# The first DMA requests of a fused attention and GLU kernel: wq in two contraction halves, in turn with x tiles 2 and 3

## The chip, the cores and the metric

The kernel runs on one core of a Trainium2 chip. The metric is the device time of one execution in microseconds. Six runs of the kernel before gave a median of 232.52 us, from 232.12 to 233.14.

A core has engines that run side by side and wait for each other through semaphores: PE (matrix products, with PEld for its weight loads), DVE (vector), ACT (scalar functions), POOL, and SP, which in this kernel only issues DMA requests.

## The reference, cut to what matters

The input x has 2048 rows of 512. It is normalized, and the result goes into two branches whose outputs are multiplied and added to x:

```python
xn = _layernorm(x, axis=-1)
s = _A_ref(xn, A_wqkv, A_wo)                  # qkv = xn @ wqkv, local attention
g = _silu(_B_ref(xn, B_w_gate, B_w_up, B_w_down))   # gelu(xn @ w_gate) * (xn @ w_up) @ w_down
return x + s * g
```

The attention has 32 heads of 16; each row attends to 8 rows, at distances 0, 2, ..., 14 behind it. wqkv is 512 x 1536: 512 columns each for q, k and v. The GLU is 1792 wide. All inputs are bf16.

## The kernel before, in words

The sequence is cut into 4 blocks of 512 rows (index j), and each block into 4 tiles of 128 rows. For a block the kernel makes, in this order on PE: q, k and v; the gate and up products of the GLU, 14 chunks (`glu`); then the down projection and the output, tile by tile (`down`). Attention's elementwise products run on DVE beside these. The program order on each engine is written out by hand (line 51), so an instruction that waits holds everything behind it on its engine.

The loads are all issued by SP, at the head of the program (lines 93 to 101): x tiles 0 to 3, one request of 128 KB each (`load_x`, line 82); then wqkv in three requests of 512 KB, q's 512 columns, k's, v's (`load_w`, line 88); then x tiles 4 to 7 in one request, halves of w_gate and w_up, and the rest of x. A request for wq, wk or wv brings for each of the 128 partitions four pieces of 512 columns, one for each contraction block of 128 rows (index k in `load_w`, dk in `project`).

The start is lines 472 to 496. PE runs 17 matmuls on zeros. For each of the first four tiles DVE computes mean and variance (`first_moments`, lines 176 and 177), ACT takes a square root (line 178), DVE the reciprocal (line 183) and the normalized tile xn (line 198). PE transposes xn in four pieces into PSUM (line 207), and the result is copied to xnT, by ACT for tiles 0 and 1 (line 216) and by DVE for tiles 2 and 3 (line 218). Tile 1's copy has two parts: contraction blocks 0 and 1, then 2 and 3.

DVE's order at the start is: moments of tiles 0 and 1, normalization of 0 and 1 (PE's transposes go beside it), then moments of tiles 2 and 3, then normalization of 2 and 3.

The first QKV matmuls (lines 486 to 489, through `project`, line 241) make q for tiles 0 and 1, 256 columns of rows at once, in four PSUM buffers: first contraction blocks 0 and 1 for all four outputs, eight matmuls, then blocks 2 and 3 for all four, eight more:

```python
    for dks in ((0, 1), (2, 3)):
        for fo in range(NC):
            project(qs[fo], wqkv_sb, fo * P, 0, 0, HQ, dks)
```

Then come the transposes of tile 2, the first k output, the transposes of tile 3, the other k outputs for tiles 0 and 1 (lines 492 to 496), q and k for tiles 2 and 3, and v for all four tiles (lines 500 to 505). The q and k results are copied to SBUF by ACT (lines 259 and 262). v goes through memory (lines 265, 267) and comes back in another layout (`load_v`, line 275).

Of the kernel before, what the change touches and what calls it, by code (L numbers as in the profile page):

```python
# [13 lines left out]
P = 128  # L14
# [14 lines left out]
def kernel(  # L29
# [14 lines left out]
    B, S, D = A_x.shape  # L44
    DF = B_w_gate.shape[1]
    NT, NC, NF, NJ = S // P, D // P, DF // P, S // TQ
    TPQ = TQ // P
# [27 lines left out]
    wqkv_sb = wts.tile([P, NC, 3 * D], BF16, name="wqkv_sb")  # L75
# [6 lines left out]
    def load_x(t, n=1):  # L82
        nc.sync.dma_start(  # L83
            out=x_sb[:, t : t + n, :],
            in_=x2d[t * P : (t + n) * P, :].rearrange("(t p) d -> p t d", p=P),
        )

    def load_w(dst, src, lo, hi):
        nc.sync.dma_start(
            out=dst[:, :, lo:hi], in_=src.rearrange("(k p) n -> p k n", p=P)[:, :, lo:hi]  # L90
        )

    for t in range(TPQ):
        load_x(t)
    for i in range(3):
        load_w(wqkv_sb, A_wqkv, i * D, (i + 1) * D)
    load_x(TPQ, TPQ)
    for i, (lo, hi) in enumerate(((0, DF // 2), (DF // 2, DF))):
        load_w(wg_sb, B_w_gate, lo, hi)
        load_w(wu_sb, B_w_up, lo, hi)  # L100
        load_x((2 + i) * TPQ, TPQ)

    def load_late_weights():
# [15 lines left out]
        out=vT.rearrange("(k p) n -> p k n", p=P)[:, :, 0:PAD],  # L119
        in_=warm[:, 0 : NC * PAD].rearrange("p (k n) -> p k n", k=NC),  # L120
# [426 lines left out]
```

The softmax here doesn't subtract the row's maximum and nothing guards it: scores larger than these inputs give would overflow.

## Time and profile before

| | |
|---|---|
| median of six runs | 232.52 us (232.12 to 233.14) |
| profiled execution: its time | 232.24 us |
| its span, first to last instruction | 230.5 us |
| PE busy | 225.0 us (98%) |
| DVE busy | 146.9 us (64%) |
| ACT busy | 132.2 us (57%) |
| granted PE clock | 0.999 |

Times inside the span count from its start. A line of a timeline gives start, duration, engine, line of the kernel, operation, what is written from what, the number of instructions merged into the line, and in square brackets how long the engine was idle before it and what ended that. The chain of waits is followed back from the last instruction: at each step to what released it. Durations of consecutive instructions on one engine overlap a little, since an engine starts one before the last is out of it.

SP's requests at the start, from the timeline: the four x tiles go out from 0.80 to 2.62 us, the three parts of wqkv from 2.66 to 4.19, x tiles 4 to 7 at 4.23, the first half of w_gate at 4.78, the first half of w_up at 5.44.

### The profile page before, as it was taken

The numbers are of one execution on the slowest core, as the hardware profiler recorded it, in microseconds if no ns is written. First come the engines' busy times: TensorE is split into PE (matmuls) and PEld (weight loads), VectorE is DVE, ScalarE is ACT, GpSimd is POOL, SyncE is SP. The second block draws the span as 40 slices with busy tenths as digits, with TensorE's granted clock in tenths as the row PEclk, the third lists the DMA queues.
The fourth block names the chain that finished last, engine by engine and source line by source line (L and its number), as shares of the span: only waits on it lengthen the run. The fifth ranks groups of instructions, "written<-read, shape, count | busy, mean of one in ns | idle before, by whom it ended". The sixth has DMA issues, their size and how long they took to land.

```text
span 230.5 us, 3545 instructions
## 1 busy us (share of the span) xinstructions
PE 225.0 (98%) x1339; PEld 106.3 (46%) x1339; DVE 146.9 (64%) x234; ACT 132.2 (57%) x219; POOL 22.1 (10%) x61
## 2 busy tenths in 40 slices
PE   7999999999999999999999999999999999999993
PEld 5865444444444444444444444444444444444453
DVE  5693996897795198981677149951449429864132
ACT  3779869755413865756621595656741386576211
POOL 1058933000000000130000000000000000000000
PEclk9999999999999999999999999999999999999999
DMA  5999499821378211100277611000046810000001
GB/s 167 362 375 367 108 214 216 278 69 48 103 173 200 50 29 23 26 0 0 92 173 163 140 24 31 18 11 0 28 136 160 203 30 0 0 0 4 23 23 46
DMA packets 27057, 23.71 MB, mean 103 GB/s; under 512 B 6688, under 2 KB 27040, under 8 KB 27040
## 3 DMA queue, kind: packets, MB, share of 16 engines
q1 hardware_dynamic: 27040, 23.49, 38.7%
q8 instruction: 10, 0.16, 0.3%
q14 instruction: 7, 0.06, 0.1%
HBM read 18.22 MB, written 4.21 MB: 97 GB/s over the span
## 4 chain that ended last, share of the span: by engine, by line
PE 93%; DVE 3%; DMA 2%; SPq 1%; ACT 0%; issue 0%; DVEq 0%
PE g_ps L241 21%; PE y_ps L398 21%; PE u_ps L241 20%; PE qkv_ps L241 17%; PE s_ps L408 6%; PE L_ps L297 3%; PE o_ps L357 3%; DVE pv L343 2%; DMA wqkv_sb<-in_A_wqkv_dram 2%; SPq L83 1%; PE tr L207 1%; DVE h L386 0%; PE sp_ps L332 0%; PE den_ps L317 0%; ACT ge L382 0%
## 5 line engine op out<-in xcount | busy, mean ns | idle before, releaser
L241 PE MATMUL g_ps<-xnT,wg_sb 128*128 128x512 bf16 x224 | 57.6, 379 | 0.0
L241 PE MATMUL u_ps<-xnT,wu_sb 128*128 128x512 bf16 x224 | 57.5, 379 | 0.0
L398 PE MATMUL y_ps<-wd_sb,h 128*128 128x512 bf16 (+1 forms) x238 | 51.2, 366 | 0.0
L386 DVE TENSOR_TENSOR h<-ge,u 128x512 bf16<-128x512 bf16 x56 | 23.7, 424 | 34.1 <-ACT u L384 33.9
L287 DVE TENSOR_TENSOR pk<-q_sb,k_sb 128x2048 bf16<-128x2048 bf16 x32 | 37.8, 1220 | 11.5 <-ACT k_sb L262 11.5
L241 PE MATMUL qkv_ps<-xnT,wqkv_sb 128*128 128x512 bf16 (+1 forms) x224 | 43.0, 349 | 0.4 <-DMA wqkv_sb<-in_A_wqkv_dram 0.4
L382 ACT ACTIVATE ge<-g_ps 128x512 bf16<-128x512 f32 x56 | 33.6, 601 | 14.4 <-PE g_ps L241 12.9
L384 ACT ACTIVATE u<-u_ps 128x512 bf16<-128x512 f32 x56 | 33.6, 600 | 13.9 <-PE u_ps L241 13.9
L343 DVE TENSOR_TENSOR pv<-E,v_arr 128x2048 bf16<-128x2048 bf16 x32 | 38.6, 1216 | 0.0
L405 ACT ACTIVATE sl<-y_ps 128x512 bf16<-128x512 f32 (+1 forms) x17 | 9.7, 572 | 44.0 <-PE y_ps L398 44.0
L398 PEld LDWEIGHTS <-h 128*128 128x128 bf16 x238 | 23.3, 98 | 25.3
L241 PEld LDWEIGHTS <-wu_sb 128*128 128x128 bf16 x224 | 21.9, 98 | 26.6 <-issue 0.3
L241 PEld LDWEIGHTS <-wg_sb 128*128 128x128 bf16 x224 | 20.8, 98 | 26.7 <-issue 4.2
L241 PEld LDWEIGHTS <-wqkv_sb 128*128 128x128 bf16 x224 | 21.5, 98 | 19.9 <-issue 0.7
L416 DVE TENSOR_TENSOR m<-s_ps,sl 128x512 bf16<-128x512 f32 (+1 forms) x17 | 11.2, 658 | 26.2 <-PE s_ps L408 26.2
L408 PE MATMUL s_ps<-wo_sb,oT 128*128 128x512 bf16 (+1 forms) x68 | 16.6, 366 | 0.0
L192 POOL TENSOR_TENSOR rstd<-rstd,mhalf 128x1 f32<-128x1 f32 x12 | 8.0, 665 | 79.3 <-DVE rstd L189 77.1
L259 ACT ACTIVATE q_sb<-qkv_ps 128x512 bf16<-128x512 f32 (+1 forms) x20 | 9.9, 513 | 5.3 <-PE qkv_ps L241 5.1
L265 ACT ACTIVATE vst<-qkv_ps 128x512 bf16<-128x512 f32 x16 | 9.6, 597 | 5.6 <-PE qkv_ps L241 5.6
L262 ACT ACTIVATE k_sb<-qkv_ps 128x512 bf16<-128x512 f32 (+1 forms) x20 | 10.2, 512 | 3.6 <-PE qkv_ps L241 3.2
L369 DVE TENSOR_TENSOR oT<-o_ps,rb 128x1024 bf16<-128x1024 f32 x8 | 9.7, 1218 | 1.4 <-PE o_ps L357 1.4
L408 PEld LDWEIGHTS <-oT 128*128 128x128 bf16 x68 | 6.6, 98 | 7.2
(49 smaller groups left out, 117.9 us busy)
## 6 DMA issues: line engine op xcount, KB each, us to landing
v_arr<-vT SPq DMA_DIRECT2D x16, 520.0 KB, 5.1
vT<-vst SPq DMA_DIRECT2D x16, 128.0 KB, 1.7
out_dram<-o_t SPq DMA_DIRECT2D x15, 128.0 KB, 2.3
wg_sb<-in_B_w_gate_dram SPq DMA_DIRECT2D x2, 896.0 KB
wu_sb<-in_B_w_up_dram SPq DMA_DIRECT2D x2, 896.0 KB, 13.5
wd_sb<-in_B_w_down_dram SPq DMA_DIRECT2D x1, 1792.0 KB, 16.8
wqkv_sb<-in_A_wqkv_dram SPq DMA_DIRECT2D x3, 512.0 KB, 5.1
x_sb<-in_A_x_dram SPq DMA_DIRECT2D x3, 512.0 KB, 9.7
```

What stands on the lines that cost most here:

```text
L241: nc.tensor.matmul(ps[:], lhsT=w[:, dk, lo : lo + P], rhs=xnT[j][:, dk, i0 : i0 + n], start=(dk == 0), stop=(dk == NC - 1),)
L259: nc.scalar.activation(out=st[j]["q"][:, c, i0 : i0 + n], in_=ps[:], func=AF.Copy)
L262: nc.scalar.activation(out=k_sb[:, c, lo : lo + n], in_=ps[:], func=AF.Copy)
L287: nc.vector.tensor_tensor(out=pk[:], in0=st[j]["q"][:], in1=k_sb[:, :, off : off + TQ], op=ALU.mult)
L343: nc.vector.tensor_tensor(out=pv[:], in0=st[j]["E"][:, wh, :].unsqueeze(1).to_broadcast([P, 4, TQ]), in1=st[j]["va"][:, 4 * g : 4 * g + 4, ...
L369: nc.vector.tensor_tensor(out=st[j]["oT"][:, 2 * gg : 2 * gg + 2, :], in0=st[j]["o"][:], in1=st[j]["rb"][:].unsqueeze(1).to_broadcast([P, ...
L382: nc.scalar.activation(out=ge[:], in_=g_ps[:], func=AF.Gelu_apprx_tanh)
L384: nc.scalar.activation(out=u[:], in_=u_ps[:], func=AF.Copy)
L386: nc.vector.tensor_tensor(out=h[:], in0=ge[:], in1=u[:], op=ALU.mult)
L398: nc.tensor.matmul(y[:], lhsT=st[j][fc][:, tt * P : (tt + 1) * P], rhs=wd_sb[:, fc, cols], start=(fc == 0), stop=(fc == NF - 1),)
L408: nc.tensor.matmul(s[:], lhsT=st[j]["oT"][:, g, tt * P : (tt + 1) * P], rhs=wo_sb[:, g, cols], start=(g == 0), stop=(g == NC - 1),)
L416: nc.vector.tensor_tensor(out=m[:], in0=s[:], in1=sl[:, cols], op=ALU.mult)
```

## The change

The first seven requests become eight. q's columns of wqkv are requested in two halves of 256 KB, contraction blocks 0 and 1, then blocks 2 and 3. The first half goes ahead of x tile 2, the second between x tiles 2 and 3. The requests for k's and v's columns and all later ones follow in their old order. The same bytes go to the same places; no engine but SP has an instruction more or less.

```diff
-    def load_w(dst, src, lo, hi):
+    def load_w(dst, src, lo, hi, k0=0, k1=NC):
         nc.sync.dma_start(
-            out=dst[:, :, lo:hi], in_=src.rearrange("(k p) n -> p k n", p=P)[:, :, lo:hi]
-        )
-
-    for t in range(TPQ):
-        load_x(t)
-    for i in range(3):
+            out=dst[:, k0:k1, lo:hi],
+            in_=src.rearrange("(k p) n -> p k n", p=P)[:, k0:k1, lo:hi],
+        )
+
+
+    load_x(0)
+    load_x(1)
+    load_w(wqkv_sb, A_wqkv, 0, D, 0, 2)
+    load_x(2)
+    load_w(wqkv_sb, A_wqkv, 0, D, 2, 4)
+    load_x(3)
+    for i in range(1, 3):
         load_w(wqkv_sb, A_wqkv, i * D, (i + 1) * D)
     load_x(TPQ, TPQ)
```

## The prediction

> **What bounds the kernel now.** I read the page's parts on busy time and groups first, then the chain of waits, then the first ten microseconds engine by engine. PE is busy for 225.0 of 230.5 us, and the chain runs along PE for 93% of the span. The one place on PE where a load ends the wait is the group of QKV matmuls:
>
> ```profile
> L241 PE MATMUL qkv_ps<-xnT,wqkv_sb 128*128 128x512 bf16 (+1 forms) x224 | 43.0, 349 | 0.4 <-DMA wqkv_sb<-in_A_wqkv_dram 0.4
> ```
>
> The columns are busy us, mean ns of one, and idle time before with its releaser: 0.41 us in the finer timeline. The chain in order of time (start us, us, what) shows where that is and what follows:
>
> ```profile
> 2.18 0.43 SPq L83
> 2.61 0.04 issue
> 2.66 4.04 DMA wqkv_sb<-in_A_wqkv_dram
> 6.69 0.05 issue
> 6.74 1.92 PE qkv_ps L241 x16
> 8.66 0.22 PE tr L207 x4
> 8.88 0.44 PE qkv_ps L241 x4
> 9.32 0.22 PE tr L207 x4
> 9.54 8.26 PE qkv_ps L241 x60
> ...
> 41.36 0.88 PE g_ps L241 x4
> 42.24 0.02 issue
> 42.26 0.60 ACT ge L382
> 42.87 0.41 DVE h L386
> 43.28 1.14 DVE pv L343
> ```
>
> The chain begins with SyncE issuing four x tiles, then waits for wq, and from 6.74 it is PE without a hole until 42.24. There it passes through DVE to 48.5 and returns to PE. That DVE stretch starts from a PE result (g_ps, then ge on ACT, then h), and the sums at 48.54 wait 0.27 us for it. DVE's idle before the h's of this stretch is ended by ACT's copies of PE results, so the stretch moves with PE. A microsecond won at 6.74 therefore should reach the end undiminished, unless another load is late.
>
> **What can start at 6.74 instead.** The first matmuls need the transposed tiles 0 and 1 as well. On ACT and DVE (start us, us, line, operation):
>
> ```profile
> 5.63 1.18 ACT L216 ACTIVATE xnT<-tr 128x512 bf16<-128x512 bf16 x3 [0.66 <-PE tr L207]
> 6.43 0.38 ACT L216 ACTIVATE xnT<-tr 128x256 bf16<-128x256 bf16 x1
> ```
> ```profile
> 2.94 0.69 DVE L176 BATCH_NORM_STATS2 stats<-x_sb 128x6 f32<-128x512 bf16 x1 [1.84 <-DMA x_sb<-in_A_x_dram]
> 5.57 0.69 DVE L176 BATCH_NORM_STATS2 stats<-x_sb 128x6 f32<-128x512 bf16 x1
> 6.39 0.66 DVE L176 BATCH_NORM_STATS2 stats<-x_sb 128x6 f32<-128x512 bf16 x1
> 7.35 0.41 DVE L198 TENSOR_SCALAR xn<-x_sb,mv,rstd 128x512 bf16<-128x512 bf16 x1
> ```
>
> ACT's three copies end at 6.23 (tile 0: 5.63 + 0.60), 6.53 (blocks 0 and 1 of tile 1: 6.15 + 0.38) and 6.81 (blocks 2 and 3: 6.43 + 0.38). Blocks 0 and 1 are all that the first eight matmuls read. So with wq in place PE could begin at 6.53 plus 0.04 to 0.06 of handing over (6.70 to 6.74 after the DMA; 5.13 to 5.19 from xn to its transpose): 6.58. **Gain at most 6.74 - 6.58 = 0.16 us**, not the 0.41 of idle time, because ACT is 0.16 us behind the load. ACT's copies go back to x tile 0's landing at 2.94, and tiles 0 and 1 are still the first two requests, so that chain stays.
>
> **The loads, one by one.** SyncE's issues and the landings (issue time plus time to landing): wq 2.66 + 4.0 = 6.70 by the chain, wk 3.13 + 5.1 = 8.23, wv 3.68 + 6.0 = 9.68, x tiles 4 to 7 4.23 + 7.0 = 11.23. The distances are 1.45 to 1.55 us per 512 KB, some 350 GB/s: the queue moves bytes in order and, from 5 us on, without pause (364 to 389 GB/s in the half-microsecond stretches to 7.0). Before that it moves 227 to 264 GB/s from 2.0 to 4.0, and only 115 to 184 from 4.0 to 5.0, where the weights follow the x tiles.
>
> First half of wq: requested third, at about 1.71 (x tile 2's old place). It ends at byte 512 KB of the queue, where x tile 3 ended. Lower bound: a lone tile's 2.14 us (0.80 to 2.94), 3.9. Upper bound: whole wq's landing, 6.70, which has twice the bytes ahead. 6.70 minus 1.45 for 512 KB gives 5.25; I take that. It is needed at 6.53: 1.3 us to spare.
>
> Second half: requested fifth, ends at byte 896 KB; needed after eight matmuls (half of the sixteen in 1.92 us), about 7.5, and cannot plausibly land behind 6.70, the landing of byte 1024 KB. Hidden.
>
> x tile 2: ends at byte 640 KB; 5.25 + 128 KB at 1.45 us per 512 KB = 5.6, against the 5.57 at which DVE is free for it. Hidden within 0.1. x tile 3: last of the same 1024 KB that ended with wq, so 6.70; DVE now takes it at 6.39. The two first_moments stand ahead of both normalizations in DVE's order, so tile 2's xn is held by tile 3 as well: it ends at 7.35 + 0.41 + 0.31 = 8.07. PE's next need:
>
> ```profile
> 6.74 1.64 PEld L241 LDWEIGHTS <-wqkv_sb 128*128 128x128 bf16 x16 [0.57 <-DMA wqkv_sb<-in_A_wqkv_dram]
> 8.39 0.32 PEld L207 LDWEIGHTS <-xn 128*128 128x128 bf16 x4
> 8.66 0.37 PEld L241 LDWEIGHTS <-wqkv_sb 128*128 128x128 bf16 x4
> ```
>
> PE turns to tile 2's transposes at 8.39, and 0.16 earlier, 8.23, after the change. Ready at 8.07 + 0.06 = 8.13: hidden with 0.10 us to spare. That is the thinnest cover of the sum: **x tile 3 may land as late as 6.80**; each later tenth costs a tenth. ACT's square root of tile 3 (7.31, then 7.62 + 0.29 = 7.91) stands ahead of the q copies, which move from 8.04 to 7.88: late by 0.03, and nobody waits that closely for them.
>
> wk: PE wants it at 8.66 - 0.16 = 8.50; it landed at 8.23. One more request stands ahead of it on SyncE (0.43 to 0.51 us each), but the bytes ahead are the same, and the queue that brings it is full: 0 is the row nearest, 0.47 the other end (8.70). At 0 it is hidden by 0.27.
>
> Later requests all come one place later on SyncE. There an issue is already held for 1.4 to 2.7 us from 5.44 on because the queue is full, so an extra 0.47 disappears in that; tiles 4 to 7 are normalized by 16.7, and PE transposes the first of them at 17.64. Cost 0, at worst 0.47, which that microsecond covers. Nothing computes more or less.
>
> **Two rules set beside the rows.** The Trainium skill, page "DMA: Bandwidth & Descriptors" (sections "Anatomy of one DMA" and "Rules for kernel authors"), speaks against the split: a DMA has about 2.0 us fixed plus bytes over 436 GB/s, and transfers should be large. Its estimate for one x tile, 2.3 us, fits the 2.14 above. If the 2.0 were paid in series by the added request, x tile 3 would land at 8.70 and tile 2's transposes would wait until 10.13, +1.74 us, 233.98. The landings 1.5 us apart above say it is overlapped, so it enters the sum as nothing. The same page ("Queues, rings and completion order") warns that completion need not follow issue order, which would make the gain 0; the four landings here are in order.
>
> **The sum.** -0.16 + 0 + 0 + 0 = -0.16 us. Profiled run: 232.24 - 0.16 = 232.08. That run lies 0.28 under the median of six (232.52); against the median the change gives **232.36 us**, 0.07% less. A measurement of this kernel can tell about 0.2% (0.47 us) from no change, so this reads as the same time.
>
> **Rivals.**
> 1. *Gain hidden by the next load.* x tile 3 lands at 6.96, or wk 0.47 later at 8.70 with its matmuls at 8.75 instead of 8.72: about 0, 232.5. For it: the issue order really puts both later. Against: equal bytes ahead of both.
> 2. *Slower: changing between x and weights costs the queue.* Between 4.0 and 5.0 it moved about 0.15 MB (115 and 184 GB/s) where 0.26 fits at the rate before; that is a loss of about 0.4 us at one change from x to weights. The new order changes from one to the other five times in place of once ahead of wk. If two of the extra ones cost 0.35 each, x tile 3 lands at 7.40, tile 2's xn ends at 8.77, PE's transposes start at 8.83 instead of 8.39: +0.44, 232.96. It decides from 6.96 on. Against: 1 KB pieces, in the same queue, either way, and a backlog that grows early.
> 3. *More than 0.16.* If PE's end of waiting is not held by ACT as the records have it, the whole 0.41 goes: 232.11. The records' ends are sharp to some hundredths, so this is unlikely.
> 4. *The change doesn't do what it says*: if the first matmuls wait for both halves (a wait kept for the whole of wq), they start when byte 896 KB lands, 6.70 - 0.36 = 6.34, still before 6.53: again -0.16, the same as my forecast. It cannot be told apart by the time.
>
> **How the numbers follow.** Forecast (with rival 4) 0.52, rival 1 0.22, rival 2 0.16, rival 3 0.10. Medians of six spread from 232.12 to 233.14, so some 0.2 us of scatter lies on each. The range takes in rivals 1 and 3 and nearly all of 2: 231.9 to 233.0. Faster by over 0.2% (below 232.05) needs rival 3 with scatter, or the forecast with much of it: 0.14. Slower by over 0.2% (above 232.99) needs half of rival 2 and some scatter: 0.14. The same: 0.72.
>
> **What the new profile would show.** Right: the 0.4 on the QKV group is no longer ended by the wqkv load but by ACT's xnT, at about 0.25; QKV starts at 6.58; transposes of tile 2 load at 8.23; the second statistics of line 176 after 5.57 start near 6.70; a steady 0.16 us less at 17.64 and 42.24. Wrong: a new wait of PE for xn (rival 2) or for wqkv_sb at the k matmuls (rival 1), or a shift that is there at 9.5 and gone by 48.5, where a load-bound DVE stretch would have swallowed it.

## The result, and the profile after

The change makes the kernel slower: 233.39 us in the median of 17 runs (232.54 to 233.91), against 232.59 for the kernel before (38 runs); the medians lie 0.80 us apart. The ratio, taken from the runs that are not in the chip's slower state, is 1.0026, with a 95% interval from 1.0014 to 1.0039: by 0.0026 x 232.59, 0.6 us slower (0.3 to 0.9). The profiled execution took 233.48 us, its span is 231.8. It is 1.24 us longer than the profiled execution of before, twice the difference that the ratio gives; why is told below, under e3 and e4.

The chain of waits of the changed kernel, from the start (start us, us, what):

```profile
2.69 0.43 SPq L89
3.13 0.04 issue
3.17 0.47 SPq L83
3.64 0.04 issue
3.68 6.32 DMA wqkv_sb<-in_A_wqkv_dram
9.99 0.05 issue
10.04 0.61 PE qkv_ps L247 x4
10.65 0.22 PE tr L213 x4
10.88 8.26 PE qkv_ps L247 x60
19.13 0.22 PE tr L213 x4
```

The load that ends PE's wait is no longer wq's but wk's, the request issued at 3.68. It took 6.32 us to land where wk's took 5.1 before. The four matmuls after it are the first k output, at 10.04 where they stood at 8.72 before (PE's record of them in the kernel before stands below this paragraph). The 60 QKV matmuls behind them start at 10.88 instead of 9.54, 1.34 later, and the span is 1.3 longer: what is lost here is not won back.

```profile
8.72 0.60 PE L241 MATMUL qkv_ps<-xnT,wqkv_sb 128*128 128x256 bf16 x4
```

PE's weight loads of the changed kernel, and DVE's first statistics and normalization (start us, us, line, operation, idle time before and what ended it):

```profile
6.81 0.15 PEld L247 LDWEIGHTS <-wqkv_sb 128*128 128x128 bf16 x1
7.17 1.62 PEld L247 LDWEIGHTS <-wqkv_sb 128*128 128x128 bf16 x15 [0.21 <-issue]
8.99 0.23 PEld L213 LDWEIGHTS <-xn 128*128 128x128 bf16 x4 [0.20 <-DVE xn L204]
10.04 0.33 PEld L247 LDWEIGHTS <-wqkv_sb 128*128 128x128 bf16 x4 [0.82 <-DMA wqkv_sb<-in_A_wqkv_dram]
```
```profile
5.62 0.68 DVE L182 BATCH_NORM_STATS2 stats<-x_sb 128x6 f32<-128x512 bf16 x1
...
7.54 0.69 DVE L182 BATCH_NORM_STATS2 stats<-x_sb 128x6 f32<-128x512 bf16 x1 [1.02 <-DMA x_sb<-in_A_x_dram]
...
8.53 0.41 DVE L204 TENSOR_SCALAR xn<-x_sb,mv,rstd 128x512 bf16<-128x512 bf16 x1
```

There are two new waits. DVE waits 1.02 us for x tile 3, so tile 2's xn is late and its transposes load at 8.99, after 0.20 us of waiting for it. And PE's weight load waits 0.82 us for wk. In this execution the first is hidden behind the second. It is not nothing by itself: with wk in time the k matmuls could have begun at about 9.22, behind the transposes (they start at 9.00 and take 0.22 in the chain), still 0.50 later than before.

What the queue did (busy time of each engine, granted clock, share of the DMA engines, GB/s), before and after:

```profile
4.00:5.00 1.00, 0.93 (x5) 0.32 (x3) 0.93 (x4) 0.53 (x2) 0.00 (x0) 1.00 0.69 150
5.00:6.00 1.00, 0.81 (x13) 0.74 (x14) 0.96 (x4) 0.37 (x1) 0.00 (x0) 1.00 1.06 373
6.00:7.00 1.00, 0.59 (x9) 0.40 (x7) 0.96 (x3) 0.99 (x4) 0.00 (x0) 1.00 1.09 386
```
```profile
4.00:5.00 1.00, 0.93 (x5) 0.32 (x3) 0.93 (x4) 0.56 (x2) 0.00 (x0) 1.00 1.01 246
5.00:6.00 1.00, 0.76 (x8) 0.77 (x9) 0.96 (x4) 0.13 (x2) 0.00 (x0) 1.00 0.52 138
6.00:7.00 1.00, 1.00 (x11) 0.96 (x10) 0.48 (x2) 0.74 (x2) 0.00 (x0) 1.00 0.74 246
```

Read the last two columns. Before, the queue was full from 5 us on (373, 386 GB/s). After, the DMA engines are busy for half of the time from 5 to 6 and for three quarters from 6 to 7, although SP had issued wk at 3.68 and wv at 4.16: work had been requested, and part of the engines' time went by without any.

A request ends in sixteen semaphore increments, one for each share. The times of the first and the last of them, from the two traces (us from the span's start), show that some shares fell behind the others:

```
                   before: issue  first share  last share    after: issue  first  last
wq, or its 2nd half         2.66     6.29         6.69               2.69   5.41   7.19
x tile 3                    2.18     4.18         4.42               3.17   5.75   7.51
wk                          3.13     7.79         8.21               3.68   7.71   9.99
wv                          3.68     9.30         9.71               4.16   9.13  11.48
```

wk's first share lands as early as before (7.71, 7.79). Its last lands 1.8 us later, because the sixteen shares have come apart: 0.4 us from first to last before, 2.3 after. The kernel waits for the last one.

### The profile page after: what moved, and what is told of

It is laid out like the page before. It is cut to its first block, busy times and chain, and to the rows that moved or that the text cites. A ratio compares the mean times of both kernels' runs of the same rounds, so it can differ in the third digit from the quotient of the medians.

```text
span 231.8 us, 3546 instructions
## 1 busy us (share of the span) xinstructions
PE 226.0 (98%) x1339; PEld 107.1 (46%) x1339; DVE 147.1 (63%) x234; ACT 132.2 (57%) x219; POOL 22.2 (10%) x61
## 4 chain that ended last, share of the span: by engine, by line
PE 91%; DVE 3%; DMA 3%; SPq 1%; issue 0%; POOL 0%; DVEq 0%
PE y_ps L404 21%; PE g_ps L247 21%; PE u_ps L247 20%; PE qkv_ps L247 16%; PE s_ps L414 6%; PE L_ps L303 3%; PE o_ps L363 3%; DMA wqkv_sb<-in_A_wqkv_dram 3%; DVE pv L349 2%; SPq L83 1%; DVE h L392 1%; PE tr L213 0%; PE sp_ps L338 0%; SPq L89 0%; PE den_ps L323 0%
```

## The experiments

Three theories stood at first. A: each change between x and weights in the queue costs (this is rival 2). B: an added request ahead of wk costs. C: the late landings of one profile are chance. All ratios are against runs of the kernel before on the same chip; the rows "before" and "the change" are e4 and e3.

```
order of requests up to wk                              number  ratio   95% interval
before      x0 x1 x2 x3 wq wk                              6     1.0007  0.9997 to 1.0017
the change  x0 x1 qa x2 qb x3 wk                           7     1.0035  1.0013 to 1.0057
e1          x0 x1 x2 x3 qa qb wk                           7     1.0018  1.0003 to 1.0033
e2          x0 x1 wq x2 x3 wk                              6     1.0006  0.9997 to 1.0016
e11         x0 x1 qa x2 x3 qb wk                           7     1.0032  1.0017 to 1.0047
e5          x0 x1 qa x23 qb wk                             6     0.9982  0.9960 to 1.0004
e12, again  x0 x1 qa x23 qb wk                             6     0.9988  0.9972 to 1.0004
e8          x0 x1 wq x23 wk                                5     1.0022  1.0013 to 1.0031
e13         x0 x1 x23 wq wk                                5     0.9986  0.9976 to 0.9997
e15, again  x0 x1 x23 wq wk                                5     0.9974  0.9953 to 0.9994
```

qa and qb are the halves of wq; x23 is tiles 2 and 3 in one request. "Number" counts the requests up to and including wk. With wv it is one more, and by that count the expectations call the kernel before seven and the change eight.

**e1, split only.** Against the changed kernel:

```diff
     load_x(1)
-    load_w(wqkv_sb, A_wqkv, 0, D, 0, 2)
     load_x(2)
-    load_w(wqkv_sb, A_wqkv, 0, D, 2, 4)
     load_x(3)
+    load_w(wqkv_sb, A_wqkv, 0, D, 0, 2)
+    load_w(wqkv_sb, A_wqkv, 0, D, 2, 4)
```

> x tiles 0 to 3 first as before, then wq in its two halves: eight requests, but only one change from x to weights. Theory A (each change between x and weights in the queue leaves some of a request's sixteen shares behind, and the request counts as landed with the last of them): one change as before, so about 232.5 us, and wk lands near 8.2. Theory B (the added request is what costs, its issue or its smaller size): like the changed kernel, about 233.3, and wk lands near 10. Theory C (the slow landings of the changed kernel's profile are chance of one execution, and the medians differ for another reason): no say on this run, 232.5 to 233.4.

Measured: 1.0018, in two groups, five runs from 231.95 to 232.73 and seven from 233.11 to 233.65. The profile caught one of the first (232.23), with wk's last share at 8.72. So the split costs without any added change between x and weights, in most runs though not in all. Against A; B is half right.

**e2, order only.**

```diff
     load_x(1)
-    load_w(wqkv_sb, A_wqkv, 0, D, 0, 2)
+    load_w(wqkv_sb, A_wqkv, 0, D)
     load_x(2)
-    load_w(wqkv_sb, A_wqkv, 0, D, 2, 4)
     load_x(3)
```

> x tiles 0 and 1, wq whole, x tiles 2 and 3, wk, wv: seven requests as before, three changes between x and weights. Theory A: between the two kernels or like the changed one, 232.9 to 233.4 us, with shares of some request in the first 10 us more than 1 us apart. Theory B: like before, 232.5, or 0.16 less, since wq is early and no request is added. Theory C: 232.4 to 232.6.

Measured: 1.0006. Three changes between x and weights, and no loss that can be told from none; in the profile x tile 3's last share landed at 6.65, where rival 2 had put it at 7.40. By the time A has fallen, and rival 2's price with it. One sign that the expectation gave to A did show: wk's shares lie 1.39 us apart in this profile (7.73 to 9.12), without any added request, and the k matmuls, ready at about 8.99, began at 9.16.

**e3 and e4, the two kernels again.**

> The changed kernel once more. Theories A and B: 233.2 to 233.5 us, k's matmuls again wait for wk, which lands after 9 us. Theory C: the wait for wk is absent or under 0.3 us in this profile.

> The kernel before once more, for a second profile and the scatter of the comparison: ratio 1.000 within 0.0015. Theories A and B: wk lands at 8.0 to 8.5 us again, no wait of PE for k's weights. Theory C: wk's landing is as scattered as the changed kernel's, some executions near 10 us.

Measured: 1.0035 and 1.0007. In e3's profile (233.04) x tile 3's last share lands at 7.56 and wk's at 9.56; in e4's, wk's lands at 8.79 and PE doesn't wait for it. The changed kernel is slower again, so the difference of the medians is no chance. But wk's landing does scatter from execution to execution: 8.79 in e4 is behind the 8.0 to 8.5 that A and B expected. And in e3 PE's own wait for wk is 0.16 us, under the 0.3 that the expectation gave to C; the larger wait there, 0.58, is for tile 2's xn, which x tile 3 held up. Without the late wk the k matmuls of e3 could have begun at about 9.27 (9.05 and 0.22). The profiles of one kernel also differ in something else. PE's transposes and first matmuls in e3, then in e4:

```profile
5.17 0.40 PE L213 MATMUL tr<-ident,xn 128*128 128x128 bf16 x4 [0.71 <-DVE xn L204]
...
6.56 1.91 PE L247 MATMUL qkv_ps<-xnT,wqkv_sb 128*128 128x256 bf16 x16 [0.25 <-ACT xnT L222]
9.05 0.40 PE L213 MATMUL tr<-ident,xn 128*128 128x128 bf16 x4 [0.58 <-DVE xn L204]
9.60 0.61 PE L247 MATMUL qkv_ps<-xnT,wqkv_sb 128*128 128x256 bf16 x4 [0.16 <-DMA wqkv_sb<-in_A_wqkv_dram]
```
```profile
5.19 0.61 PE L207 MATMUL tr<-ident,xn 128*128 128x128 bf16 x4 [0.26 <-DVE xn L198]
...
7.33 1.92 PE L241 MATMUL qkv_ps<-xnT,wqkv_sb 128*128 128x256 bf16 x16 [0.49 <-ACT xnT L216]
...
9.31 0.60 PE L241 MATMUL qkv_ps<-xnT,wqkv_sb 128*128 128x256 bf16 x4
```

The four transposes take 0.40 us in one execution and 0.61 in the other. In the traces the first record of a granted PE clock of 1.0 begins at 3.85 us in e3 and at 6.45 in e4. At the slow rate ACT's copies come later: blocks 0 and 1 of xnT are there at 7.04 in e4 instead of 6.53 before. Its QKV starts later still, at 7.33. The profile names ACT, whose last copy (blocks 2 and 3) ends at 7.31; but the first eight matmuls don't read those blocks, and wq's last share landed at 7.29. It is the execution that differs, not the kernel: the changed kernel has 0.61 in its first profile and 0.40 in e3. The first profile of before had the higher rate and an early wq, so that its k matmuls began at 8.72, against 9.31 in e4. The first profile of after had a later wk than e3, 9.99 against 9.56; its lower rate cost nothing, since PE waited for wk. That is why the two first profiles lie 1.24 us apart and the medians less.

One sum ties all profiles together. The time of the profiled execution less the start of the first k output is 223.52 us before (232.24 - 8.72), 223.50 in e4, 223.44 in e3 and 223.44 after (233.48 - 10.04); over all fourteen profiled executions of kernels that compute, those below included, it lies between 223.44 and 223.60. So what an order of requests costs or gains, it costs or gains ahead of that matmul.

**e5 and e12, halves kept, x tiles 2 and 3 in one request.**

```diff
-    load_x(2)
+    load_x(2, 2)
     load_w(wqkv_sb, A_wqkv, 0, D, 2, 4)
-    load_x(3)
```

> x tiles 0 and 1, first half of wq, x tiles 2 and 3 in one request, second half, wk, wv: seven requests as in the kernel before, with wq still in halves and still in turn with x. Theory B1 (an eighth request in front of wk, with its issue of 0.47 us, is the cost): as before, 232.5 to 232.7 us, wk's last share by 8.8. Theory B2 (short requests at the front leave the queue without a reserve, so that the engines wait at the head of each next request, wherever it stands): as the changed kernel, 233.0 to 233.5, wk's last share after 9.

> x tiles 0 and 1, first half, x tiles 2 and 3 in one request, second half, once more, for a narrower interval. If seven requests with the halves are as good as the kernel before: ratio 0.999 within 0.002. If the earlier ratio was chance of that chip: 1.001 or more.

Measured: 0.9982 and 0.9988, both intervals with 1 in them. The loss is gone with wq still in halves and in turn with x. By the time, this is B in its first form: one request fewer ahead of wk is enough. The landings are less clear. wk's last share came at 8.80 in e5's profile, and at 9.38 in e12's (232.95, the second longest of its eleven runs), where PE waited for it:

```profile
9.43 0.61 PE L246 MATMUL qkv_ps<-xnT,wqkv_sb 128*128 128x256 bf16 x4 [0.63 <-DMA wqkv_sb<-in_A_wqkv_dram]
```

So a late wk occurs in this order too. How much of it the early first half of wq makes up for (QKV started at 6.92 and 6.67) is not separated.

**e6, wv in halves instead of wq.**

```diff
-    for i in range(1, 3):
-        load_w(wqkv_sb, A_wqkv, i * D, (i + 1) * D)
+    load_w(wqkv_sb, A_wqkv, D, 2 * D)
+    load_w(wqkv_sb, A_wqkv, 2 * D, 3 * D, 0, 2)
+    load_w(wqkv_sb, A_wqkv, 2 * D, 3 * D, 2, 4)
```

(ahead of it x tiles 0 to 3 and wq whole, as before)

> The kernel before with wv, the seventh request, in two contraction halves instead of wq: eight requests, the added one behind wk. Theory B1 in the form that any added request costs: 233.0 or more. Theory B1 in the form that it must stand ahead of wk, and theory B2 (the queue has its reserve by then): as before, 232.4 to 232.8, wk's last share by 8.8.

Measured: 0.9993 (0.9976 to 1.0011), wk's last share at 8.39. An added request behind wk costs nothing that can be told from none.

**e7, the change with wk requested by ACT.** 

```diff
-    for i in range(1, 3):
-        load_w(wqkv_sb, A_wqkv, i * D, (i + 1) * D)
+    load_w(wqkv_sb, A_wqkv, 2 * D, 3 * D)
...
     nc.scalar.activation(out=std[:, 0, :], in_=epsc[:], func=AF.Sqrt, bias=epsc[:], scale=1.0)
+    load_w(wqkv_sb, A_wqkv, D, 2 * D, eng=nc.scalar)
```

> The changed kernel with wk requested by ACT (after its first square root, near 2.4 us) instead of SP. If the wait of the k matmuls for wk is what carries the loss to the end, it is gone and the time is 232.4 to 232.7; x tile 3 may then be the next, late by some tenths. If the loss is carried by something else (x tile 3, the transposes, the clock), it stays at 233.0 to 233.4.

Measured: 1.0086 (1.0055 to 1.0117), outside both expectations. Its chain:

```profile
3.17 5.21 DMA x_sb<-in_A_x_dram
8.38 0.02 issue
8.41 0.70 DVE stats L182
```

ACT issued wk at 3.38, not near 2.4, so only 0.30 us ahead of SP's 3.68 in the change. It landed at 9.87, no earlier than in e3, and x tile 3 at 8.38. x tile 3 became the bound, and the wait that the run was to remove was replaced rather than removed. It doesn't show what carried the loss.

**e8, wq whole, then x tiles 2 and 3 in one request.**

```diff
     load_x(1)
-    load_w(wqkv_sb, A_wqkv, 0, D, 0, 2)
-    load_x(2)
-    load_w(wqkv_sb, A_wqkv, 0, D, 2, 4)
-    load_x(3)
+    load_w(wqkv_sb, A_wqkv, 0, D)
+    load_x(2, 2)
```

> x tiles 0 and 1, wq whole, x tiles 2 and 3 in one request, wk, wv: six requests, the order of the change without its halves. Theories B1 and B2 both: not slower than before, 232.2 to 232.6 us, wk's last share at 8.0 to 8.6, because fewer and larger requests stand ahead of it; faster than before by at most the 0.16 us that ACT's copies leave.

Measured: 1.0022, against the expectation. Tiles 2 and 3 land together at 7.41 in its profile, behind wq. DVE needs tile 2 at 5.6 and takes both only now, one after the other; the k matmuls start at 9.92. Few requests do not help if one with an early use stands behind a large one.

**e11, x tile 3 ahead of the second half.** 

```diff
     load_x(2)
-    load_w(wqkv_sb, A_wqkv, 0, D, 2, 4)
     load_x(3)
+    load_w(wqkv_sb, A_wqkv, 0, D, 2, 4)
```

> x tiles 0 and 1, first half of wq, x tile 2, x tile 3, second half, wk, wv: eight requests as in the change, with x tile 3 and the second half exchanged. If x tile 3's place (DVE's statistics, then tile 2's transposes) carries the loss, it is gone: 232.4 to 232.7. If an eighth request ahead of wk carries it, it stays: 233.0 to 233.5.

Measured: 1.0032. Its chain:

```profile
3.65 6.06 DMA wqkv_sb<-in_A_wqkv_dram
9.71 0.05 issue
9.75 0.61 PE qkv_ps L247 x4
```

x tile 3's last share landed at 6.02, early enough, and the loss is the same: wk at 9.71 ends the last wait, and x tile 3 isn't needed for the loss. It isn't wk alone either. In this order the second half of wq landed at 8.17, and PE waited 0.60 us for it in the middle of the q matmuls; with wk in time the k matmuls could have begun at about 9.31 (9.09 and 0.22) instead of 9.75. What is common to both is a last share that comes late.

**e9 and e10, the load heads alone.** A kernel without computation issues the requests up to the first part of w_up, waits until all has landed, and begins again, 24 times, in four orders in turn.

> No computation: only the head of the load queue, 24 times one after the other, each time after everything has landed, in four orders in turn, six times each: as before, as changed, split only (x 0 to 3, two halves of wq), pair (x 0, x 1, first half, x 2 and 3 in one, second half). The output is not computed. Measured is, from the first issue, when the last share of x tile 3 and of wk has landed. Theory B (the order and the number of requests make wk late): medians of wk as in the profiles, changed later than before by 0.8 to 1.5 us, split between, pair 0.3 to 0.6 later. Theory F (the first touch of each part of the source in a program is what stalls single pieces): only the first one or two repetitions are slow, and from the third on all orders land wk within 0.5 us of each other, earlier than in the profiles. Theory C (chance): medians of all orders within 0.3 us, with single repetitions 1 us late in every order.

> The same with the four orders taken in another sequence, so that another order stands first in the program; the output is not computed. Theory B: the medians of the first such run again, within 0.3 us. Theory F: the slow first repetition is now one of another order. Theory C: the order of the medians changes.

Measured over both, twelve repetitions of each order, in us from the first issue (add 0.80 for the span's time in the kernel):

```
order                        x tile 3, last    wk, first   wk, last: median (lowest to highest)
before                            3.63           6.94            7.79   (7.52 to 8.51)
the change                        6.94           7.04            8.82   (8.11 to 9.40)
split only (e1)                   3.91           6.85            8.87   (7.71 to 9.43)
halves, x 2 and 3 in one (e5)     4.70           6.59            8.35   (7.57 to 9.14)
```

This speaks for B: the split alone makes wk's last share 1.08 us later, as much as the whole change (1.03), while the first share stays. The last repetitions are as slow as the first, so it is not the first touch of the source (theory F of the expectation), and the two runs agree on the sequence of the four (7.62, 8.35, 8.62, 8.76 and 7.87, 8.34, 8.92, 8.95: before, in one, change, split), so it isn't chance. The count of requests isn't all of it: the last order has as many as the kernel before, and its wk comes 0.56 us later.

**e14, from six to ten requests.** The same, in the order x, wq, wk; six has x 2 and 3 in one request, small has a further request of 16 KB between wq and wk, eight has wq in halves, ten in quarters.

> No computation, the output is not computed: the head of the load queue again, 30 times, in five orders, six times each. All keep the order x, wq, wk, wv; six has x 2 and 3 in one request, seven is as before, small is seven with one more request of 16 KB between wq and wk, eight has wq in halves, ten has wq in quarters. If the count of requests is the cost: wk's last share, from the first issue, 7.4 (six), 7.8 (seven), 8.8 (small and eight), 10 or more (ten). If the halving is the cost and not the count: small as seven, eight 8.8, ten later still. If neither: all within 0.3 us.

```
requests    wk, first   wk, last: median (lowest to highest)   pieces of 1 KB slower than 150 ns
six            6.59          7.62   (7.40 to 8.34)                      37
seven          6.88          7.85   (7.50 to 8.18)                      38
small          6.92          8.38   (7.81 to 8.87)                      48
eight          7.05          9.10   (8.51 to 9.88)                      58
ten            7.31          9.00   (8.35 to 9.65)                      60
```

16 KB more of data would take 0.05 us at 350 GB/s; the small request makes wk's last share 0.53 us later in the median. So a request costs more than its bytes. Halving wq costs 1.25, and quarters cost no more than halves: neither form of the expectation holds alone. These are six repetitions of each order, and their ranges overlap; six and seven requests can't be told apart here. Nor is it the later issue of wk that decides: wk is issued 2.83 us after the first request in small and 2.80 in eight, which lie 0.72 apart, and 3.71 in ten, which is no later than eight. The last column, from the DMA records of the first 11 us of a repetition (medians), goes along with it. A 1 KB piece usually takes 46 ns; some take 150 ns to 1.7 us, and there are more of them with eight or ten requests at the head than with six or seven. In the first 11 us of the two kernels' first profiles there are 25 before and 41 after.

**e13 and e15, six requests: the version that beats both.**

```diff
-    for t in range(TPQ):
-        load_x(t)
+    load_x(0)
+    load_x(1)
+    load_x(2, 2)
     for i in range(3):
```

(against the kernel before)

> x tiles 0 and 1, x tiles 2 and 3 in one request, wq whole, wk, wv: the order of the kernel before with six requests instead of seven; wq and wk are issued 0.45 us earlier. If each request ahead of wk leaves its last share later, wq and wk land earlier than before and the QKV matmuls start nearer to 6.58: 0.2 to 0.5 us faster, 232.1 to 232.4 beside a before of 232.6. If the halving of wq is what matters, not the count: 232.4 to 232.6.

> The six requests once more, for a narrower interval and a second profile, since the first profile is that of the slowest of its runs. If six requests are faster than seven: ratio 0.998 to 0.9995 again, and in the profile wk's matmuls start before 9.1 us. If the first ratio was chance: 1.000 or more.

Measured: 232.45 beside 232.76, ratio 0.9986, and 232.23 beside 232.78, 0.9974; both intervals end below 1, 0.3 to 0.6 us faster. PE in e15's profile (232.62, at the slow rate of the transposes):

```profile
7.06 1.91 PE L245 MATMUL qkv_ps<-xnT,wqkv_sb 128*128 128x256 bf16 x16
8.81 0.39 PE L211 MATMUL tr<-ident,xn 128*128 128x128 bf16 x4
9.03 0.60 PE L245 MATMUL qkv_ps<-xnT,wqkv_sb 128*128 128x256 bf16 x4
```

wq's last share is there at 6.41 and wk's at 8.33, PE waits for neither, and the k matmuls start 0.28 us earlier than in e4 at the same rate. It isn't so in every execution: in e13's profile, the longest of its runs (233.07), wk's last share landed at 9.43 and the k matmuls at 9.47 waited 0.56 us for it. That six requests are faster than seven is measured; that wk's earlier landing makes the gain is argued, since e14 doesn't tell the two apart.

## Why the prediction was wrong

**The chain from 6.74 to the end.** Right: what is lost at the first k output (1.32 us) is lost at the end (1.3), and the sum under e3 and e4 shows the same for every profile.

**QKV could start at 6.58.** Right where the transposes ran at the rate of the first profile: 6.56 in e3, 6.58 in e1, 6.57 in e11. Not seen was that this rate differs between executions of one kernel, 0.40 to 0.61 us for four transposes, so that QKV starts at 6.56 to 7.19 even where wq is there in time (7.17 in the first profile of after, 7.19 in e8).

**Both halves of wq and x tile 2 in time.** Right as to the need: last shares at 4.70, 7.19 and 5.06. But the second half was said not to land behind 6.70, and it did, at 7.19 and, in e3, at 6.89; in e11's order it came at 8.17 and PE waited for it.

**x tile 3 at 6.70, limit 6.80.** Wrong: 7.51 and 7.56, and 7.20 or later in all twelve repetitions of the head. The price that the prediction put on it was right: 0.81 late moves tile 2's transposes from 8.13 to 8.94, and they loaded at 8.99. By itself that is some 0.5 us at the k matmuls (9.22 instead of 8.72). The wait for wk lies on top of it, and where x tile 3 was in time (e11) the loss stayed.

**wk at 8.23, or 0.47 later.** This is the step that failed, with x tile 3 beside it. The prediction held that the bytes ahead were the same and the queue full, so that 0 was the nearest row and 8.70 the other end. wk's last share came at 9.99, 9.56, and 8.91 or later in all twelve repetitions of the head, 9.62 in the median. With the same bytes ahead the first share stayed (6.94 and 7.04 in the heads, medians). But a request counts as landed with the last of its sixteen shares, and the last came 1.03 later. The trace of before may have had a sign of it: the queue's 115 to 184 GB/s between 4 and 5 us, which the prediction read as a loss at the change from x to weights, a price that e2 didn't find. That shares fell behind there is not shown.

With 9.62 in place of 8.70 the k matmuls begin at 9.67. That is 0.95 later than the 8.72 that the prediction had for the kernel before, and 0.65 later than the middle of 8.72 and 9.31, its two profiles. Measured: 0.6 by the ratio, 0.8 between the medians. The size fits, but the middle was taken afterwards and from two executions, so this is an estimate and no proof.

**Rival 1** had the place, wk and the k matmuls, and took 0.47 for the delay. **Rival 2** had the sign and put x tile 3 at 7.40, near the 7.51 measured, but by a price that e2 didn't find, and with the wrong request at the end of the chain; that the number came near was luck. **Rival 3** didn't occur: QKV started at 6.56 at the earliest. **Rival 4** was said not to be tellable by the time; the profiles tell it: in e3 QKV started at 6.56 and the second half of wq landed at 6.89, so the first matmuls don't wait for both halves.

**The rule that was set aside.** The Trainium skill, page "DMA: Bandwidth & Descriptors" ("Rules for kernel authors"), asks for few and large requests. The prediction found the fixed cost overlapped and let it go. In the direction the rule is right here: six requests in front beat seven (e13, e15), though not in every order (e8), and added ones cost 0.5 to 1.25 us at wk (e14). The 2.0 us that the prediction took from the page stands there in "Anatomy of one DMA", which is about requests issued by GpSimd; here SP issues them. The first x tile's 2.11 us from issue to last share is near the 2.3 that the prediction worked out from it; no run shows 2.0 us paid once more for each added request. (The prediction's 233.98 for that case starts from the profiled run, while its forecast and its rivals start from the median; from the median it is 234.26.)

**What stays open.** Why single pieces take up to 1.7 us, and why halving costs more than a small request, isn't named by the trace. That there are more such pieces with more requests at the head is measured; that they are what holds the last shares back is not shown, nor what an engine waits for in them. In single executions wk was late in other orders too (9.12 in e2, 9.38 in e12, 9.43 in e13), so the request count shifts how often and how far, and isn't the only cause. No run has x tile 3 late and wk in time, so what each of the two costs alone is an estimate.

## What to carry to other kernels

Price a moved or split load by when its last share lands, not by the bytes ahead of it, and look at the request behind it which an engine needs next: here the gain was sought at wq and lost at wk. Before splitting a request to have part of it sooner, try to merge others ahead of it; two x tiles in one request gave what the split was meant to give, as long as they stayed ahead of the large request (e13, e15) and not behind it (e8). Where two profiles differ by more than the medians, take a second profile of each before reading the difference.

## What the runs showed of the hardware that was not expected

- The sixteen shares of one 512 KB request (wk) landed within 0.4 us of each other in one execution of the kernel before, 0.9 in another (e4), and 2.3 us apart in the changed kernel; there they stay apart, 2.28 in wk and 2.35 in wv behind it. The Trainium skill, "DMA: Bandwidth & Descriptors" ("Why a DMA increments its semaphore by 16 and not by 1"), says that the sixteen engines finish independently and that only the full count means that all has landed; the traces agree.
- A request of 16 KB ahead of a 512 KB one delayed the latter's last share by 0.53 us and its first by 0.04 (medians of six, with ranges that overlap).
- PE's rate doubles at a time that differs from execution to execution. In e4 PE's 128-column matmuls start every 107 ns up to 6.3 us and every 56 ns from 6.5 on; the trace's first record of a granted clock of 1.0 begins at 6.45 there, and between 3.85 (e3) and 6.98 us (after) in all fourteen profiles. (The views print 1.00 also ahead of that record, where the trace has none.) Four transposes beginning at 5.2 us took 0.40 us in some and 0.61 in others, after the same 17 warming matmuls. The page "TensorE: Matmul & The Clock Gate" ("Part 1: The HAM clock gate") puts this down to an activity window that runs free of the kernel's start; the runs agree that it varies, and cannot show the window.
